# Seven PSUM banks in one pool, padded 128-row fills and 40 side chunks in a fused attention and gated-MLP kernel

## The chip, the cores and the metric

The kernel runs on one core of one Trainium2 chip. What counts is its time on the device in microseconds, the median of several runs. The core has five engines with instruction queues of their own: TensorE (PE in the profile; PEld are its weight loads), VectorE (DVE), ScalarE (ACT), GpSimd (POOL) and SyncE (SP, which here only issues DMAs). The engines run side by side and wait for each other on semaphores. Matmuls write into PSUM, which has eight banks of 128 x 512 fp32; VectorE and ScalarE read it from there, and in this kernel GpSimd reads and writes SBUF alone.

## The reference

```python
def _attn_ref(x, inducing):            # x (4, 12416, 128), inducing (32, 128)
    I = np.broadcast_to(inducing[None], (B, m, C))
    def mab(q, kv):
        s = scale * (q @ kv.transpose(0, 2, 1))
        s = s - s.max(-1, keepdims=True)
        a = np.exp(s)
        a /= a.sum(-1, keepdims=True) + 1e-09
        return a @ kv
    h = mab(I, x)                       # stage 1: 32 rows attend to all of x
    return mab(x, h)                    # stage 2: every row of x attends to the 32
def _moe_ref(x, w_gate, w_val, w_out): # 49664 tokens, d_ff = 1536
    gate = 1.0 / (1.0 + np.exp(-(x @ w_gate)))
    val = x @ w_val
    return gate * val @ w_out
```

Stage 2's result is `a2 @ h` with only 32 columns in `a2`, so the kernel multiplies `h` by the gate and value weights once for each batch (`hw`, 32 rows) and gets every hidden value as `a2 @ hw`. The sigmoid is written as (tanh(z/2) + 1) / 2, and the half is taken at the end.

## The kernel before

**Tiling.** The 49664 tokens are cut into 97 blocks of 512 tokens, 24 to a batch and one of left-over columns at the end. The hidden size of 1536 is 12 slices of 128. A *chunk* is one slice of one block, 128 x 512 hidden values, and there are 1164. For each chunk TensorE makes two *fills* of one PSUM bank each (`hidden_mm`, L1080): the gate values and the value part, with 32 rows of `hw` as weights. The two slices of a pair and the gate and value parts lie on four different groups of 32 rows, so up to four fills can run beside each other in the array. ScalarE takes tanh of the gate bank into a ring in SBUF (`issue_gate`, L1131), for one chunk or two at a time. VectorE makes the *product* (t + 1) * v from the ring and the value bank (`product`, L1276), again for one chunk (128x512) or two (128x1024). TensorE then multiplies the product by `w_out` in four matmuls of 128 columns (`out_mm`, L1218), which gather all 12 slices of a block in the bank `acc`. ScalarE evacuates that bank (L1333), and SP sends the block off (L1244).

**Banks.** The eight banks are given out by tags: two for double gate fills (`g2`), one for single ones (`g1`), two for the double value fills of every other step (`v2`), two for the steps between (`vm`), and one for `acc`. Of `vm`, the second bank also takes the small work of the two attention stages and of side chunks. So gate units of two chunks (letter `g`) and of one (`h`) take turns.

**Side chunks.** Nine chunks, in the blocks that `ASIDE` lists, go another way (`plan_aside`): ScalarE takes tanh into SBUF (L1187), GpSimd adds 1 (L1189), ScalarE copies the value bank into SBUF (L1192), and GpSimd multiplies (L1194). Their output matmuls come at the end of their block.

**The attention stages** run in the gaps. For each group of 2048 columns, stage 2 makes scores on TensorE (L624), ScalarE copies them out (L661), GpSimd takes the row maximum in a tree of pairwise steps and subtracts it (L671 to L676), ScalarE takes `exp` (L685), GpSimd sums in a tree (L693), inverts (L717 to L732) and spreads the result over four row groups (L739), and SP transposes it by DMA (L750) into `a2r`, which the fills read. Stage 1 of the next batch runs at the same time: scores, maximum (L386), `exp` (L399), transposing DMA (L423), weighted sums (L434).

**The order** is a string written out by hand or by a tool, `ORDER`: a letter is one step, and all engines get their instructions in the order in which the letters issue them. `V` and `W` fill value banks, `x` is a product, `o12` twelve output matmuls, `e` an evacuation by ScalarE (`f` by VectorE), `k7` or `K7` the next step of side chain 7. Side chains are the attention stages, loads and transposes of x, and the side chunks. Steps on one engine run in that order; a step that waits holds up what is behind it.

Of the kernel before, what the change touches and what calls it, by code (L numbers as in the profile page):

```python
# [10 lines left out]
F32 = mybir.dt.float32  # L11
F16 = mybir.dt.float16
# [10 lines left out]
    75, 79, 79, 86, 91, 91, 91, 95, 95,  # L23
# [13 lines left out]
RING = 16  # L37
ORDER = """
ghVxgVxk0hk0Vxgo4hVk0xo4Vxgo12Vxho4ghk72Vxo8k0gVxo4k0k74Vxho12Wxeghk76Vxo12gWxo4hk0Vxo4go4Vxho4g
k0k73Vxk1Vxho8k1k1k1gVxhVxo12Vxegk6Vk6xho16k6gk6Vxo8hWxo4ghk83Vxo4Wxgo8hVxo8Vxeghk8o8Vk8xgk8hVx  # L40
o16gk8Vxo4Wxho8gk75Vxo12ehWxgo12hk78Vxo4k7k1gVxo4k7k7hk1Vxo8gWxo8Vxho4gWxo8ehk1k77Vxgo12hWxo4go4
hVxo4k2gVxo4k2k1k80Vxk2k2ho8gWxo12VxehVxgk10o4hVk10xo4Vxgo4ho8Vxk10go8hWxo8gk10Vxo4ho4k9gVxk9Vx
o4k9ehgWxo8hk79k82Vxo8gVxk12o4hVk12xo4Vxgo4ho8k84Vxk12go12Wxehk12Vxgo8k18k2hVk18xo12k18gk2Vxo4hV
xo12k18Vk18xgo8hWxo4eghk2k81k85Vxo12k11Vxgk11hVxo12k11gVxo4hVxo4k3gVxo4k3k2Vxk3k3ho12WxegVxho12V
xgk14hVk14xo4Vxgo20Vxk14hgWxo12k14Vxehgo4k13Vxho4k13gVxo4Vxho12Vxk13go8hWxo4go4hVxo8egVxk16hVk16
xo8k16gVxo12k16Vxk3ho8k19Vxk19go4hk3Vxo8k15gVxk15Vxk15ho8egWxk3Vxho12k17gVxo4k17hVxo4k17gVxo12h
k3Vk20k20xo4k4Vxk4go12VxehWxgo12hVxo4go4k5hVxk5k5k5gVxo8k20hWxo8k20k86k87Vxgo12ehWxgo8Vxho8gWxo8
hVxo4go4Vxho4gVxo12VxehgVxo8hVxo8Vxk5ghVxo12k5Vxgo4hVxo4k20gVk20xo8Vk20xho4eghk5Vxk21Vxk21o8k21
k21gVxo8hWxo8gVxho12gWxo12ehk5VxgVxk20o8k20hVxo4gVxo8hVxo4gWxo4ho8gVxo4Wxho8eghVxo12gWxo4hk88Vx
o8gWxo8Vxk21hgo12k20Vxo4k20ehk21VxgWxo8ho4gk21k89Vxo8hWxo4go4hk21Vxo8gWxo12ehVxgo8Wxho8gVxo8hk22  # L50
gVxk22Vxho8k22k22gVxo4hVxo12WxeghVxo16gWxo8Vxho4ghWxo8gVxo12ehVxgo4Vxho8gWxo8hVxo8k22ghWxo16k22
k90VxgWxo4ehgk22Vxo12hWxo4go4k91Vxho8gWxho8gk22Vxo4Vxho8Vxegk23Vxho8k23k23k23gk92Vxo12hWxo4gVxo8
ho4gWxo12ehk93Vxgk28o8Vk28xho8Vxk28go4Wxho4k28Vxgo8hWxo4go8hk94Vxo4Vxegk30ho12Vk30xgk30hVxo8k30V
xgo4Wxho8gk95Vxo4hk29Vxk29k29gVxho12Wxegk96Vxho16k31k23gVxo4hk23Vxk31o8k31gVxhVxo8gWxo4k23Vxho8e
# [40 lines left out]
def kernel(  # L95
# [184 lines left out]

    vm = []
    joined = {}
    OTHER = {"v1": "m", "m": "v1"}

    here = {"bank": "m"}

# [14 lines left out]
    def bank(tag, shape, dtype, name):  # L301
        if tag == "m":
            tag = here["bank"]
# [1065 lines left out]
```

## Time and profile before

| what | value |
|---|---|
| median of 3 runs | 714.05 us (713.93 to 714.75) |
| the profiled execution: its own time | 713.77 us |
| its span, first to last instruction | 712.0 us |
| granted TensorE clock | 1.0 throughout |
| products (L1276) | 484 for two chunks, 187 for one |
| tanh into the ring (L1131) | 385 for two chunks, 385 for one |
| side chunks | 9 |
| evacuations by ScalarE (L1333) | 96 |

How the profile's rows are read: a group's row has the source line, the engine, the operation, its output and input tiles with shapes, and how often it occurs; behind the first bar the busy time in us and the mean duration of one in ns; behind the second the time that the engine stood idle just ahead of them, and what ended it. A row of the waits has in us the total, how often, and the longest. A row of the timeline has start and duration in us. Consecutive instructions of DVE or ACT overlap: the next starts before the row of the last has ended, so what a step costs its engine is read from start to start.

### The profile page before, as it was taken

What the parts mean: (1) busy time and instruction counts of PE and PEld (TensorE: products, weight loads), DVE (VectorE), ACT (ScalarE), POOL (GpSimd) and SP (SyncE); (2) the same over time, 40 slices, a digit from 0 to 9 for tenths busy, and PEclk for the clock granted to TensorE, in tenths of its full rate; (3) what the DMA queues carried; (4) which work ended last, traced back from release to release, by engine and by line L of the source; (5) the groups of instructions that cost most, each with busy time, mean ns of one, the idle gap of its engine ahead of it and who ended that gap; (6) DMA issues with size and microseconds to landing.
All of it is one profiled execution on the core that took longest, in us unless ns stands there. A gap on an engine that the chain in (4) does not pass through costs nothing.

```text
span 712.0 us, 21058 instructions
## 1 busy us (share of the span) xinstructions
PE 681.4 (96%) x8446; PEld 402.0 (56%) x8446; DVE 697.3 (98%) x773; ACT 679.1 (95%) x1019; POOL 446.0 (63%) x718
## 2 busy tenths in 40 slices
PE   8899999999999999999999999999999999999997
PEld 4455565555555555555555555555555555555555
DVE  6899999999999999999999999999999999999997
ACT  4699999999999999999999999999999999999996
POOL 4574663788763747578766266378766788766220
PEclk9999999999999999999999999999999999999999
DMA  9796775244459353325258631220222222023011
GB/s 212 116 175 136 144 142 114 75 91 107 90 126 172 65 120 84 69 75 122 49 131 156 116 76 53 70 73 33 77 61 47 74 61 76 31 75 77 31 46 46
DMA packets 118178, 65.73 MB, mean 92 GB/s; under 512 B 101408, under 2 KB 102208, under 8 KB 118080
## 3 DMA queue, kind: packets, MB, share of 16 engines
q1 hardware_dynamic: 112176, 50.90, 30.4%
q0 software_dynamic: 5584, 13.34, 11.2%
q8 instruction: 66, 1.08, 0.7%
q14 instruction: 32, 0.26, 0.1%
q10 hardware_dynamic: 320, 0.15, 0.1%
HBM read 27.80 MB, written 25.43 MB: 75 GB/s over the span
## 4 chain that ended last, share of the span: by engine, by line
PE 46%; ACT 23%; DVE 20%; issue 8%; DMA 2%; POOL 1%; DVEq 0%; ACTq 0%; POOLq 0%
PE acc_ps L1218 22%; DVE u L1276 18%; ACT t L1131 18%; PE g_ps L1080 12%; PE vm_ps L1080 5%; PE v_ps L1080 4%; ACT o L1333 3%; DMA xn<-in_x_dram 2%; PE vm_ps L624 1%; PE vm_ps L434 1%; ACT sc L661 1%; ACT a1T L399 1%; DVE nm L386 1%; ACT e L685 0%; PE vm_ps L1177 0%
## 5 line engine op out<-in xcount | busy, mean ns | idle before, releaser
L1131 ACT ACTIVATE t<-g_ps 128x1024 f16<-128x1024 f32 (+1 forms) x770 | 587.8, 819 | 10.6 <-PE g_ps L1080 2.0
L1276 DVE SCALAR_TENSOR_TENSOR u<-t,v_ps 128x1024 f16<-128x1024 f16 (+1 forms) x337 | 407.6, 1210 | 0.9 <-PE v_ps L1080 0.3
L1218 PE MATMUL acc_ps<-wo,u 128*128 128x128 f16 x4596 | 364.4, 220 | 4.8 <-ACT o L1333 0.9
L1218 PEld LDWEIGHTS <-u 128*128 128x128 f16 x4620 | 262.5, 98 | 153.6 <-issue 146.3
L1276 DVE SCALAR_TENSOR_TENSOR u<-t,vm_ps 128x1024 f16<-128x1024 f16 (+1 forms) x335 | 307.6, 918 | 0.4 <-PE vm_ps L1080 0.2
L1080 PE MATMUL g_ps<-a2r,hwt 32*128 32x512 f16 (+1 forms) x1179 | 286.5, 375 | 5.1 <-ACT t L1131 0.4
L1080 PEld LDWEIGHTS <-hwt 32*128 32x128 f16 x2382 | 98.5, 91 | 116.8 <-issue 47.1
L1080 PE MATMUL v_ps<-a2r,hwt 32*128 32x512 f16 (+1 forms) x687 | 129.3, 373 | 5.2 <-DVE u L1276 3.7
L1080 PE MATMUL vm_ps<-a2r,hwt 32*128 32x512 f16 (+1 forms) x492 | 129.0, 376 | 5.0 <-DVE u L1276 3.2
L693 POOL TENSOR_TENSOR sum<-e 128x256 f32<-128x256 f16 (+1 forms) x23 | 15.5, 673 | 121.2 <-ACT e L685 117.8
L739 POOL TENSOR_TENSOR a2n<-e,rs 128x2048 f16<-128x2048 f16 (+3 forms) x25 | 86.8, 3474 | 5.1 <-DVE rs L711 3.4
L717 POOL TENSOR_TENSOR near<-sme,minus 128x16 f32<-128x16 f32 (+1 forms) x22 | 65.2, 2966 | 1.7
L1333 ACT ACTIVATE o<-acc_ps 128x512 f32<-128x512 f32 x96 | 57.8, 602 | 0.7 <-ACT t L1131 0.2
L672 POOL TENSOR_SCALAR rise<-rise 128x256 f32<-128x256 f32 (+6 forms) x110 | 51.2, 465 | 9.7
L671 POOL TENSOR_TENSOR rise<-sc 128x256 f32<-128x256 f32 (+1 forms) x22 | 16.2, 738 | 27.2 <-ACT sc L661 27.1
L673 POOL TENSOR_TENSOR top<-top,rise 128x128 f32<-128x128 f32 (+3 forms) x88 | 28.4, 323 | 7.3
L693 POOL TENSOR_TENSOR sum<-sum 128x128 f32<-128x128 f32 (+3 forms) x92 | 28.5, 309 | 7.2
L671 POOL TENSOR_TENSOR rise<-top 128x128 f32<-128x128 f32 (+3 forms) x88 | 27.3, 310 | 6.9
L1194 POOL TENSOR_TENSOR xn_spare<-xn_spare 128x512 f16<-128x512 f32 x9 | 11.4, 1270 | 22.5 <-ACT xn_spare L1192 22.3
L676 POOL TENSOR_TENSOR sc<-sc,top 128x512 f32<-128x512 f32 (+1 forms) x22 | 23.9, 1086 | 1.7
L1189 POOL TENSOR_SCALAR xn_spare<-xn_spare 128x512 f32<-128x512 f16 x9 | 13.4, 1492 | 18.3 <-ACT xn_spare L1187 18.2
L624 PE MATMUL vm_ps<-hT,xT 128*128 128x32 f16 x376 | 17.5, 177 | 0.6 <-DVE u L1276 0.3
(165 smaller groups left out, 328.2 us busy)
## 6 DMA issues: line engine op xcount, KB each, us to landing
out_dram<-o SPq DMA_DIRECT2D x96, 256.0 KB, 2.3
xn<-in_x_dram POOLq DMA_DIRECT2D x18, 512.0 KB, 6.0
xn<-in_x_dram POOLq DMA_DIRECT2D x3, 544.0 KB, 6.5
xn<-in_x_dram POOLq DMA_DIRECT2D x3, 256.0 KB, 12.1
xn<-in_x_dram SPq DMA_DIRECT2D x1, 576.0 KB, 4.8
xn<-in_x_dram SPq DMA_DIRECT2D x1, 512.0 KB, 3.9
a2r<-a2n SPq DMA_TRANSPOSE x29, 4.5
wg<-in_moe_w_gate_dram POOLq DMA_DIRECT2D x1, 384.0 KB, 12.2
```

The lines of the kernel that those rows point to most:

```text
L624: on("m", nc.tensor.matmul(s2[:, j, :], xT[b][:, c + j, :], hT16[b][:], start=(j == 0), stop=whole and j == j1 - 1, skip_group_check=True,))
L671: nc.gpsimd.tensor_tensor(out=r, in0=far, in1=near, op=ALU.subtract)
L672: nc.gpsimd.tensor_scalar_max(out=r, in0=r, scalar1=0.0)
L673: nc.gpsimd.tensor_tensor(out=top[:, 0:n, 0:w], in0=near, in1=r, op=ALU.add)
L693: nc.gpsimd.tensor_tensor(out=d[:, 0:n, :], in0=src[:, :, 0:w], in1=src[:, :, w : 2 * w], op=ALU.add)
L717: nc.gpsimd.tensor_tensor(out=near[:, 0:n], in0=sme[:, 0:n], in1=minus1[:, 0:n], op=ALU.pow)
L739: eng.tensor_tensor(out=a2n[:, 0:n, :, :], in0=e.unsqueeze(2).to_broadcast((P, n, 4, m)), in1=rs.unsqueeze(2).unsqueeze(3).to_broadcast((P ...
L1080: made_mm.append(nc.tensor.matmul(out[:, col : col + nb * P], hw[b][r : r + 32, j // 2, :], a2r[r : r + 32, o : o + nb, :].rearrange("p j ...
L1131: i = nc.scalar.activation(out=ring[:, p : p + n, :], in_=g[:, 0:n, :], func=AF.Tanh, scale=0.5)
L1218: mm = nc.tensor.matmul(acc[0][half][:, i, :], u[:, ts(i, P)], wo16[:, j, :], start=(i in fresh), stop=not left[ib] and not any(e[1] == ib ...
L1276: x = nc.vector.scalar_tensor_tensor(out=u[:, 0:n, a:e], in0=ring[:, p : p + n, a:e], scalar=1.0, in1=v[:, 0:n, a:e], op0=ALU.add, op1=ALU ...
L1333: evac.pop()(lambda out, in_, by: nc.scalar.mul(out=out, in_=in_, mul=by))
```

## The change

1. The eight banks are now one tile of seven banks (`vm`) and `acc`. Each gate and value fill names its banks in the order itself: `g01` fills banks 0 and 1 with gate values of two chunks, `v4` bank 4 with the value part of one. A side chain's step that takes a bank is written with a capital (`A` to `G` are banks 0 to 6). `on` no longer parts two banks but keeps, bank by bank, who used it last, and makes each user wait for that one alone.
2. Some fills are padded to 128 rows: `p` and `q` for gate and value fills, capitals `H` to `N` for side chains. Their weights are a copy of `hw` in which the 96 other rows are zero, and they read all 128 rows of `a2r`. GpSimd makes these weights once for each batch (`make_alone`) in a part of `xT` that stage 2 has done with: one memset of 128 x 3072 and four copies of 32 x 768. 218 fills are padded.
3. `ASIDE` lists 40 chunks instead of 9, from block 7 on instead of block 75.
4. The order is drawn anew. It has 464 products for two chunks and 196 for one, 444 tanhs into the ring for two and 236 for one, 90 evacuations by ScalarE and six (`f`) by VectorE. The places in the ring are counted round 15, with a sixteenth for a pair that would straddle the end.

The core of the diff:

```diff
 ASIDE = (
-    75, 79, 79, 86, 91, 91, 91, 95, 95,
+    7, 11, 12, 13, 24, 24, 26, 27, 32, 34, 36, 38, 48, 50, 51, 51, 53, 56, 58, 59, 61, 64, 68,
+    70, 75, 75, 79, 79, 79, 82, 84, 86, 86, 89, 90, 91, 91, 91, 95, 95,
 )
...
-ghVxgVxk0hk0Vxgo4hVk0xo4Vxgo12Vxho4ghk72Vxo8k0gVxo4k0k74Vxho12Wxeghk76Vxo12gWxo4hk0Vxo4go4Vxho4g
+g01C0k0g3v45k0g6xg0g3v1v65xg4g0o8xg1v34o4g56v0k0g1xxv34o4k74v0g56o12k0v2xg34v56xg10xxo8v23g4o12
...
+    def on(where, i, keep=()):
+        if vm:
+            banks = frozenset((here["bank"],) if where == "m" else where)
             me = str(i.ins.engine)
...
+            for (others, who), group in seen.items():
+                if who != me and not others & banks:
+                    tc.declare_no_dep(i.ins, group=group, keep=list(keep), reason="another bank")
...
+            after = {}
+            for k in banks:
+                for who, x in reversed(users.setdefault(k, [])):
+                    if who == me:
+                        break
+                    after.setdefault(x.name, x)
+                    if who == PE:
+                        break
+                users[k] = [(who, x) for who, x in users[k] if who != me] + [(me, i.ins)]
+            for name in after:
+                tc.add_manual_dep(i.ins, name, AFTER, reason="the bank's use before this one")
...
-    vm.append(ps.tile([P, 2, 512], F32, tag="vm", name="vm_ps"))
+    vm.append(ps.tile([P, 7, 512], F32, tag="vm", name="vm_ps"))
...
+    def make_alone(b):
+        w = xT[b][:, NLO : NLO + 4 * NI, :]
+        nc.gpsimd.memset(w, 0.0)
+        for r in range(4):
+            q = slice(32 * r, 32 * r + 32)
+            nc.gpsimd.tensor_copy(out=w[q, NI * r : NI * r + NI, :], in_=hw[b][q])
+        alone[b] = w
+
+    def weights(what, b, j, whole):
+        r = j % 2 + (2 if what == "v" else 0)
+        if whole:
+            return alone[b][:, NI * r + j // 2, :], slice(0, P)
+        q = slice(32 * r, 32 * r + 32)
+        return hw[b][q, j // 2, :], q
...
+    def fill_unit(what, c, banks, whole):
+        home = sorted(banks)
+        for k in banks:
+            j = c + home.index(k)
+            made_hw = [x for b, _, _ in blocks[chunks[j][0]] for x in joined.get(b, ())]
+            for i in hidden_mm(what, j, vm[0][:, k, :], whole):
+                on((k,), i, made_hw)
+        return span(vm[0], home)
...
-        g = ps.tile([P, n, 512], F32, tag=f"g{n}", name="g_ps")
-        for k in range(n):
-            hidden_mm("g", c + k, g[:, k, :])
...
+        g = fill_unit("g", c, banks, whole)
...
-        v = vm[0] if half else ps.tile([P, 2, 512], F32, tag="v2", name="v_ps")
...
+        ready.append((fill_unit("v", c, banks, whole), banks))
```

What the new table makes of the engines' queues is shown with the prediction, at the places that it speaks of: ScalarE and GpSimd around the third group of stage 2 of the first batch, and TensorE a third of the way through.

More of the change, by code (lines that the diff above doesn't have):

```diff
@@ L309, in bank @@
         size = 1
[L310 to L311 removed]
+        for n in shape[1:]:
+            size *= n
         flat = flat[:, 0:size]
```

390 lines of the change are left out of this document (211 added, 179 removed).

## The prediction

> **What bounds the kernel now.** I read the page, then the busy times by stretch, what VectorE (DVE) waited for, its products by shape, and last the timeline of one stretch. First the page's span, its busy line and engine shares of the chain that ended last, the ordered part from 40 to 690 us in the stretch view (length, then PE, PEld, DVE, ACT, POOL busy), and two rows of DVE's waits.
>
> ```profile
> span 712.0 us, 21058 instructions
> PE 681.4 (96%) x8446; PEld 402.0 (56%) x8446; DVE 697.3 (98%) x773; ACT 679.1 (95%) x1019; POOL 446.0 (63%) x718
> PE 46%; ACT 23%; DVE 20%; issue 8%; DMA 2%; POOL 1%; DVEq 0%; ACTq 0%; POOLq 0%
> 40.00:690.00 650.00, 629.02 (x7750) 370.42 (x7747) 649.33 (x678) 638.70 (x949) 425.91 (x675) 1.00 0.41 90
> DVE u L1276 <- PE v_ps L1080: 0.3, 1, 0.3
> DVE u L1276 <- ACT t L1131: 0.3, 1, 0.3
> ```
>
> Three engines look full, but only DVE is: for 650 us it stands still 0.7 us, and its two waits on the products are 0.3 us each. The chain passes through TensorE, ScalarE and DVE because they hand banks round in a ring; it doesn't name the bound. So the cost of one DVE step is what counts, from one start to the next. Its products by shape, then a stretch of the timeline (start, duration):
>
> ```profile
> L1276 DVE SCALAR_TENSOR_TENSOR u<-t,v_ps 128x1024 f16<-128x1024 f16 x335 | 406.8, 1214 | 0.9 <-PE v_ps L1080 0.3 <-ACT t L1131 0.3
> L1276 DVE SCALAR_TENSOR_TENSOR u<-t,vm_ps 128x1024 f16<-128x1024 f16 x149 | 181.0, 1215 | 0.2
> L1276 DVE SCALAR_TENSOR_TENSOR u<-t,vm_ps 128x512 f16<-128x512 f16 x186 | 126.6, 681 | 0.2 <-PE vm_ps L1080 0.2
> 304.04 1.22 DVE L1276 SCALAR_TENSOR_TENSOR u<-t,v_ps 128x1024 f16<-128x1024 f16 x1
> 305.17 0.68 DVE L1276 SCALAR_TENSOR_TENSOR u<-t,vm_ps 128x512 f16<-128x512 f16 x1
> 305.77 1.21 DVE L1276 SCALAR_TENSOR_TENSOR u<-t,v_ps 128x1024 f16<-128x1024 f16 x1
> 306.90 1.22 DVE L1276 SCALAR_TENSOR_TENSOR u<-t,vm_ps 128x1024 f16<-128x1024 f16 x1
> ```
>
> Rows overlap by 0.08 us: a double product holds DVE 1.13 us (305.77 to 306.90), a single one 0.60 (305.17 to 305.77). There are 484 doubles and 187 singles (the last is cut in two).
>
> **The change, part by part.** *DVE.* Counted in the new table, 464 doubles and 196 singles are left for 1124 chunks, and six evacuations (`f`) come to DVE. The nearest row for one of those has half its width:
>
> ```profile
> L1235 DVE TENSOR_SCALAR o<-vm_ps 128x256 f32<-128x256 f32 x1 | 0.4, 425 | 0.3 <-PE vm_ps L1218 0.3
> ```
>
> At double width it adds what 256 columns add to a product, 0.27: 0.69, or 0.61 from start to start. DVE: -20 x 1.13 + 9 x 0.60 + 6 x 0.61 = **-13.5 us**, all on the path.
>
> *ScalarE* (ACT). Its groups, then a stretch without a wait:
>
> ```profile
> L1131 ACT ACTIVATE t<-g_ps 128x1024 f16<-128x1024 f32 x385 | 397.0, 1031 | 9.8 <-PE vm_ps L1080 1.9 <-PE g_ps L1080 1.9 <-PE v_ps L1080 1.3
> L1131 ACT ACTIVATE t<-g_ps 128x512 f16<-128x512 f32 x385 | 233.4, 606 | 0.8 <-PE g_ps L1080 0.2
> L1333 ACT ACTIVATE o<-acc_ps 128x512 f32<-128x512 f32 x96 | 57.8, 602 | 0.7 <-ACT t L1131 0.2
> L1187 ACT ACTIVATE xn_spare<-vm_ps 128x512 f16<-128x512 f32 x9 | 5.4, 601 | 0.0
> L1192 ACT COPY xn_spare<-vm_ps 128x512 f32<-128x512 f32 x9 | 5.3, 586 | 0.0
> 102.85 1.02 ACT L1131 ACTIVATE t<-g_ps 128x1024 f16<-128x1024 f32 x1
> 103.77 0.58 ACT L661 COPY sc<-vm_ps 128x512 f32<-128x512 f32 x1
> 104.23 0.61 ACT L1131 ACTIVATE t<-g_ps 128x512 f16<-128x512 f32 x1
> 104.72 0.62 ACT L1333 ACTIVATE o<-acc_ps 128x512 f32<-128x512 f32 x1
> 105.20 1.54 ACT L1131 ACTIVATE t<-g_ps 128x1024 f16<-128x1024 f32 x2
> ```
>
> From start to start a double tanh is 0.92, a single 0.49, a copy 0.46, an evacuation 0.48. The new table has 444 doubles and 236 singles. With 31 more side chunks (a tanh and a copy each): 59 x 0.92 - 149 x 0.49 + 31 x 0.95 - 6 x 0.48 = **+7.9 us**. Priced so, the 949 ACT steps between 40 and 690 need about 614 of 650 us; the rest of its 638.7 "busy" is ends that nothing overlapped. After: 622 of 650 - 13.5 = 636.5, where DVE needs all: 97.7% where it was 94.5%. On ACT, around the third `exp` (`e<-sc`) of the first batch; `xn` is a side chunk's room; before, then after:
>
> ```order
> L399 ACTIVATE a1T<-vm_ps,nm_1_143 128x512
> L1131 ACTIVATE t_621<-g_ps 128x1024
> L685 ACTIVATE e<-sc 128x512
> L1131 ACTIVATE t_621<-g_ps 128x512
> L449 COPY hst_146<-vm_ps 32x129
> L1131 ACTIVATE t_621<-g_ps 128x1024
> ```
>
> ```order
> L1257 ACTIVATE xn_1632<-vm_ps 128x512
> L1262 COPY xn_1632<-vm_ps 128x512
> L1202 ACTIVATE t_619<-vm_ps 128x1024 x3
> L1407 ACTIVATE o_2141<-acc_ps 128x512
> L490 COPY hst_146<-vm_ps 128x129 x2
> L1257 ACTIVATE xn_1632<-vm_ps 128x512
> L727 ACTIVATE e<-sc 128x512
> L1202 ACTIVATE t_619<-vm_ps 128x512
> L1262 COPY xn_1632<-vm_ps 128x512
> ```
>
> Where double and single tanhs took turns, three doubles now stand in a row, and two side chunks stand close together, one of them round the `exp`; every tanh behind them in ACT's queue comes later by their 1.9 us, which the tanhs ahead of DVE must cover. If they don't, the 1.9 us stand on the path.
>
> The six `f` evacuations hand their output transfers to SP after DVE instead of ACT; an output is waited for by nothing but the end, so I cost that at nothing (256 KB each; if SP's queue stood behind one, the transposes in it would come later by a product, 1.13).
>
> *GpSimd* (POOL). A side chunk's two steps, the bounds for the padded weights, and its two largest waits:
>
> ```profile
> L1189 POOL TENSOR_SCALAR xn_spare<-xn_spare 128x512 f32<-128x512 f16 x9 | 13.4, 1492 | 18.3 <-ACT xn_spare L1187 18.2
> L1194 POOL TENSOR_TENSOR xn_spare<-xn_spare 128x512 f16<-128x512 f32 x9 | 11.4, 1270 | 22.5 <-ACT xn_spare L1192 22.3
> L218 POOL MEMSET ones<- 128x128 f32 x1 | 0.2, 224 | 0.0
> POOL sum L693 <- ACT e L685: 117.8, 19, 14.3
> POOL rise L671 <- ACT sc L661: 27.1, 12, 3.5
> ```
>
> 31 x 2.76 = 86 us. A batch's padded weights (a memset of 3072 columns, four copies of 768) lie between 5 x 0.22 = 1.1 us and 6144 columns at 1492/512 ns = 17.9; I take 5.5, nearer the memset, as nothing is computed: 22 us for four. POOL goes from 446 to about 554 of 700; the 145 us in the two waits cover the 108. On POOL behind the third maximum tree (which ends in `sc`), before, then after:
>
> ```order
> L676 TENSOR_TENSOR sc<-sc,top 128x512
> L693 TENSOR_TENSOR sum_2522<-e 128x256
> L693 TENSOR_TENSOR sum_2524<-sum_2522 128x128
> L693 TENSOR_TENSOR sum_2526<-sum_2524 128x64
> L693 TENSOR_TENSOR sum_2528<-sum_2526 128x32
> ```
>
> ```order
> L718 TENSOR_TENSOR sc<-sc,top 128x512
> L1259 TENSOR_SCALAR xn_1632<-xn_1632 128x512
> L1264 TENSOR_TENSOR xn_1632<-xn_1632 128x512
> L1259 TENSOR_SCALAR xn_1632<-xn_1632 128x512
> L735 TENSOR_TENSOR sum_2245<-e 128x256
> L735 TENSOR_TENSOR sum_2247<-sum_2245 128x128
> ```
>
> 4.3 us of side work (1.49 + 1.27 + 1.49) stand where POOL waited for `exp`. Behind them queue the sums and the spread, behind those on SP the transposing DMA that later fills wait for, and behind the last of them in PE's queue the side chunk's own output products, with every fill after those. The side chunks of the first two batches use the room of `xn` of the batches after next, so the loads into it, which POOL issues, wait for those products; they are needed a batch later, some 170 us, and cost nothing unless POOL stands on them. The Trainium skill (GPSIMD Engine Reference, 4.1 Engine selection) speaks against this: elementwise work belongs on VectorE, GpSimd being about 2x slower with two inputs and near line rate with one. The trace has the one-input step slower (1.49) than the two-input one (1.27); priced by the page, 0.53 + 1.2 instead of 2.76, the 86 us would be some 54, and the end would not move.
>
> *TensorE* (PE). Fills and output products (start, duration), and the only 128-row matmuls of 512 columns near them:
>
> ```profile
> 300.25 0.40 PE L1218 MATMUL acc_ps<-wo,u 128*128 128x128 f16 x4
> 300.58 0.39 PE L1080 MATMUL g_ps<-a2r,hwt 32*128 32x512 f16 x2
> 300.78 0.39 PE L1080 MATMUL v_ps<-a2r,hwt 32*128 32x512 f16 x2
> 301.10 0.62 PE L1218 MATMUL acc_ps<-wo,u 128*128 128x128 f16 x8
> 301.65 0.39 PE L1080 MATMUL g_ps<-a2r,hwt 32*128 32x512 f16 x1
> 29.22 0.82 PE L329 MATMUL w_ps<-xT,ident 128*128 128x512 f16 x3
> ```
>
> Three padded-size matmuls take 0.82 - 0.39 = 0.43 up to the last start: 0.22 each. 128 columns cost (0.55 - 0.33) / 4 = 0.055; four and a change of shape 0.33, so a change is 0.11, and two 32-row fills up to the next change 0.32 = 0.22 + 0.10. Walked over PE's order, the changes fall from 1370 to 1189 (-18 us), and 218 of 2304 fills become padded, which run alone: were all to ride beside another now, +48; by the walk they give back the 18 and 2 more (609 us before, 611 after). Either way PE needs under 640 of 698, hidden by DVE. The Trainium skill (TensorEngine Tiling (Array Packing), Tiling Modes, Key Properties) says that a change of tiling mode drains TensorE; the trace agrees, at 0.11 a change. Also, waits for a bank now stand on the weight load. PE a third of the way through, with the engine that each waits for, before, then after (`xT` holds padded weights, `hwt` the old ones):
>
> ```order
> L1080 LDWEIGHTS hwt
> L1080 MATMUL g_ps<-a2r,hwt 128x512 [waits Activation_49]
> L1080 LDWEIGHTS hwt
> L1080 MATMUL g_ps<-a2r,hwt 128x512
> L1080 LDWEIGHTS hwt
> L1080 MATMUL v_ps<-a2r,hwt 128x512 [waits DVE_49]
> ```
>
> ```order
> L1145 LDWEIGHTS xT_97 [waits DVE_49]
> L1145 MATMUL vm_ps<-a2r,xT_97 128x512
> L1145 LDWEIGHTS xT_97
> L1145 MATMUL vm_ps<-a2r,xT_97 128x512
> L1145 LDWEIGHTS xT_97 [waits Activation_49]
> L1145 MATMUL vm_ps<-a2r,xT_97 128x512
> ```
>
> All four fills are padded here, and some 1400 waits moved to the loads; behind each stands the whole PE queue, as before. A load that waited, in before:
>
> ```profile
> 40.40 0.11 PEld L1218 LDWEIGHTS <-u 128*128 128x128 f16 x2 [0.36 <-DVE u L1276]
> 40.41 0.23 PE L1218 MATMUL acc_ps<-wo,u 128*128 128x128 f16 x1 [0.19 <-DVE u L1276]
> ```
>
> Its matmul followed 0.01 us later: a load that may not run ahead costs between 0 (it can't gain) and its row's 0.11, and I take 0.01, the row that shows it. Only stalled fills pay it, and PE's spare 87 us hide it.
>
> **The sum.** 712.0 - 13.5 = 698.5 span, + 1.8 around it (713.8 - 712.0) = 700.3 if DVE stays as full. By needs in stretches of 24 chunks, ACT or PE now tops DVE in 8 of 48 stretches, by 2.9 us together, of which DVE lost 0.7; after, in 14 of 47, by 9.3: a quarter is 2.2, and 1 us for late GpSimd work: **703.5 us**. The run is 0.3 under the median of 714.05.
>
> **The rivals.** *ACT becomes the bound* (22%). The best stretch of before:
>
> ```profile
> 550.00:650.00 100.00, 96.73 (x1120) 56.70 (x1116) 99.92 (x102) 99.13 (x148) 77.88 (x116) 1.00 0.23 61
> ```
>
> Its 148 ACT steps, priced as above, fill 96.6%, with DVE still full. If that is the most that ACT can be fed, its 622 us take 643.9 instead of 636.5: 707.7, and at 96% 711.7. For it: a tanh can't start before PE has refilled a bank that ACT or DVE has just left, and the banks are as many as before (seven besides the accumulator's). Against: in before DVE's pace held ACT back, so 96.6% is no limit that it ran into, and 149 fewer single tanhs mean fewer hand-overs.
>
> *GpSimd is late, and the kernel slower* (13%). The margin of an `exp` behind its tree:
>
> ```profile
> 507.14 1.08 POOL L676 TENSOR_TENSOR sc<-sc,top 128x512 f32<-128x512 f32 x1
> 509.61 0.63 ACT L685 ACTIVATE e<-sc 128x512 f16<-128x512 f32 x1
> ```
>
> The tree ended at 508.22, 1.4 us before. The added 108 us of POOL are 4.9 for each of 22 groups. If ACT stands 1.6 at each `exp`, a third of that, the tanhs queued behind it lose 35 us; ACT's spare 14.5 takes some, 20.5 are left, and less the 13.5 won it is 7 slower: 721. It decides from (14.5 + 13.5) / 22 = 1.3 us per `exp`. For it: the margin is small already, and ACT has little to catch up with. Against: the order was redrawn, and POOL's waits hold more than the added work.
>
> *It doesn't do what it says* (7%): the seven banks are one tile, and where a fill still waits for another bank's user the two rings fall into step; by a wait of half a product's time at one in 24 products, 27 x 0.57 = 15, the gain is gone: 714. *All of it fits* (8%): the stretches cost nothing and DVE's rows close up: 699.5.
>
> **The numbers.** The forecast has 50% and by itself reaches from 700 (nothing lost) to 707 (7 of the stretches' 9.3 us paid in full). From 699 to 712.5 the range takes in it, the full gain and ACT as the bound, 80%; it leaves out no change and the slower case. A measurement tells 0.2% (1.4 us): faster 0.80, same 0.07, slower 0.13.
>
> **What would show it.** Right: 464 and 196 products at the old durations, DVE near 684 us busy and idle for under 4 between 40 us and the last 20; 444 and 236 main tanhs; POOL near 550 us; PE below DVE. ACT as the bound would show as DVE waiting for `t`, late GpSimd work as ACT's `exp` waiting for `sc` or output products waiting for `xn`, a load that costs as DVE waiting for fills. What would make the forecast wrong is several us of any of these three, or products that became slower beside a busier GpSimd.

## The result, and the profile after

The changed kernel takes 709.26 us (median of 4 executions, 708.05 to 710.49), the kernel before, measured beside it, 713.99; the ratio is 0.9932 (95% interval 0.9911 to 0.9954). It is 4.7 us faster, where 10.5 were forecast. The profiled execution took 708.05 us, the shortest of the four. First the page of the changed kernel: span, engines, shares of the chain that ended last; then the stretch view from 40 to 690 us and two of DVE's waits.

```profile
span 706.2 us, 21185 instructions
PE 679.1 (96%) x8446; PEld 402.2 (57%) x8446; DVE 687.7 (97%) x768; ACT 676.7 (96%) x985; POOL 553.2 (78%) x800
PE 62%; ACT 18%; DVE 9%; issue 5%; DMA 4%; POOL 1%; DVEq 0%; ACTq 0%; POOLq 0%
40.00:690.00 650.00, 632.97 (x7817) 374.68 (x7817) 645.46 (x679) 641.56 (x919) 531.47 (x755) 1.00 0.41 90
DVE u L1344 <- ACT t L1202: 1.4, 2, 1.2
DVE u L1344 <- PE vm_ps L1145: 0.9, 3, 0.4
```

DVE no longer fills the stretch: it stands for 4.54 us (650 - 645.46) where it stood for 0.67. The chain has moved from DVE (20% to 9%) to TensorE (46% to 62%). The groups of DVE and ACT by shape, and GpSimd's padded weights:

```profile
L1344 DVE SCALAR_TENSOR_TENSOR u<-t,vm_ps 128x1024 f16<-128x1024 f16 x463 | 539.9, 1213 | 2.9 <-PE vm_ps L1145 0.9
L1344 DVE SCALAR_TENSOR_TENSOR u<-t,vm_ps 128x512 f16<-128x512 f16 x196 | 129.3, 679 | 1.5 <-ACT t L1202 1.4
L1409 DVE TENSOR_SCALAR o<-acc_ps 128x512 f32<-128x512 f32 x6 | 4.1, 686 | 0.0
L1202 ACT ACTIVATE t<-vm_ps 128x1024 f16<-128x1024 f32 x444 | 441.8, 1046 | 6.9 <-PE vm_ps L1145 3.8
L1202 ACT ACTIVATE t<-vm_ps 128x512 f16<-128x512 f32 x236 | 139.2, 623 | 1.3 <-PE vm_ps L1145 0.5
L1129 POOL COPY xT<-hwt 32x768 f16<-32x768 f16 x16 | 13.1, 818 | 0.8
L1126 POOL MEMSET xT<- 128x3072 f16 x4 | 10.6, 2658 | 0.2
```

463 doubles and the cut last one, 196 singles, six `f`, all at the old durations: DVE's work fell as forecast. So 13.5 us of work went and 5.8 of span. DVE's busy sum fell by only 9.6 (697.3 to 687.7): a product whose successor comes late shows its last 0.08 us as busy, which an overlapped one hides. By this reckoning 13.5 - 9.6 = 3.9 us of overlap were lost, and DVE stood still 3.9 us more. That is 7.8 us, where the sum had 3.2.

The 7.8 us are mostly short stops. One of them, in TensorE's and then DVE's part of the timeline (start, duration):

```profile
441.29 1.05 PE L1288 MATMUL acc_ps<-wo,u 128*128 128x128 f16 x16
442.27 0.40 PE L1145 MATMUL vm_ps<-a2r,hwt 32*128 32x512 f16 x4
441.98 0.68 DVE L425 TENSOR_REDUCE nm<-vm_ps 128x1 f32<-128x512 f32 x1
442.80 2.35 DVE L1344 SCALAR_TENSOR_TENSOR u<-t,vm_ps 128x1024 f16<-128x1024 f16 x2
```

DVE's reduction ended at 442.66, the product began at 442.80: its fill stood behind 16 output products in TensorE's queue. The longest stop is another. Its rows are SP's issues, the wait of TensorE and the spreads on GpSimd; the first fence is the changed kernel, the second the kernel before, where the same transposition went out ten us sooner:

```profile
209.25 8.02 SPq L197 DMA_TRANSPOSE xT<-xn  x3
218.49 1.22 SPq L464 DMA_TRANSPOSE a<-a1T  x1
219.80 1.93 SPq L792 DMA_TRANSPOSE a2r<-a2n  x1
210.65 3.61 POOL L781 TENSOR_TENSOR a2n<-e,rs 128x2048 f16<-128x2048 f16 x1
PE vm_ps L1145 <- DMA a2r<-a2n: 1.0, 1, 1.0
```

```profile
206.02 3.61 POOL L739 TENSOR_TENSOR a2n<-e,rs 128x2048 f16<-128x2048 f16 x1
209.66 1.90 SPq L750 DMA_TRANSPOSE a2r<-a2n  x1
```

The spread ended 4.6 us later than before (214.26 to 209.63), behind the side chunks on GpSimd, and then its DMA was issued only 5.5 us later (219.80): SP's queue still held the last of the three transposing DMAs of the input (to 217.27), an output and a transposing DMA of weights (`a<-a1T`). TensorE waited 1.0 us at 224 us, ACT for it, and DVE for ACT: the 1.2 in DVE's first wait above.

### The profile page after: what moved, and what is told of

It reads as the page before. It is cut to its first block, busy times and chain, and to the rows that moved or that the text cites. A ratio compares the mean times of both kernels' runs of the same rounds, so it can differ in the third digit from the quotient of the medians.

```text
span 706.2 us, 21185 instructions
## 1 busy us (share of the span) xinstructions
PE 679.1 (96%) x8446; PEld 402.2 (57%) x8446; DVE 687.7 (97%) x768; ACT 676.7 (96%) x985; POOL 553.2 (78%) x800
## 4 chain that ended last, share of the span: by engine, by line
PE 62%; ACT 18%; DVE 9%; issue 5%; DMA 4%; POOL 1%; DVEq 0%; ACTq 0%; POOLq 0%
PE acc_ps L1288 30%; PE vm_ps L1145 27%; ACT t L1202 14%; DVE u L1344 8%; ACT o L1407 2%; PE vm_ps L1247 2%; DMA xn<-in_x_dram 2%; PE vm_ps L666 1%; DMA xT<-xn 1%; DMA a2r<-a2n 1%; PE vm_ps L413 0%; ACT xn_spare L1262 0%; ACT sc L703 0%; PE vm_ps L475 0%; DMA a<-a1T 0%
## 5 line engine op out<-in xcount | busy, mean ns | idle before, releaser
L1344 DVE SCALAR_TENSOR_TENSOR u<-t,vm_ps 128x1024 f16<-128x1024 f16 (+2 forms) x661 | 651.6, 1053 | 4.4 <-ACT t L1202 1.4
L1202 ACT ACTIVATE t<-vm_ps 128x1024 f16<-128x1024 f32 (+1 forms) x680 | 557.3, 899 | 8.2 <-PE vm_ps L1145 4.3
L1145 PE MATMUL vm_ps<-a2r,hwt 32*128 32x512 f16 (+1 forms) x2103 | 281.6, 377 | 12.1 <-DVE u L1344 4.4
L1145 PEld LDWEIGHTS <-hwt 32*128 32x128 f16 x2127 | 82.3, 91 | 114.8 <-ACT t L1202 29.5
L1145 PE MATMUL vm_ps<-a2r,xT 128*128 128x512 f16 x193 | 62.6, 382 | 1.5 <-DVE u L1344 0.4
L1259 POOL TENSOR_SCALAR xn_spare<-xn_spare 128x512 f32<-128x512 f16 x28 | 41.8, 1494 | 17.2 <-ACT xn_spare L1257 16.9
L1264 POOL TENSOR_TENSOR xn_spare<-xn_spare 128x512 f16<-128x512 f32 x28 | 35.6, 1270 | 19.1 <-ACT xn_spare L1262 10.5
L1145 PEld LDWEIGHTS <-xT 128*128 128x128 f16 x193 | 16.3, 97 | 17.2 <-DVE u L1344 5.4
L1259 POOL TENSOR_SCALAR xn<-xn 128x512 f32<-128x512 f16 x12 | 17.9, 1495 | 8.0 <-ACT xn L1257 7.7
L1247 PE MATMUL vm_ps<-a2r,hwt 32*128 32x512 f16 x55 | 20.1, 383 | 0.3 <-DVE u L1344 0.2
```

The lines of the kernel that those rows point to most:

```text
L1145: made_mm.append(nc.tensor.matmul(out[:, col : col + nb * P], w, a2r[q, o : o + nb, :].rearrange("p j t -> p (j t)"), start=True, stop=True,))
L1202: i = on(banks, nc.scalar.activation(out=span(ring, spots), in_=g, func=AF.Tanh, scale=0.5), [x for q in old for x in product_of[q]])
L1247: on("m", nc.tensor.matmul(st[what], w, a2r[q, o : o + nb, :].rearrange("p j t -> p (j t)"), start=True, stop=True,))
L1259: nc.gpsimd.tensor_scalar_add(out=st["t1"], in0=st["t"], scalar1=1.0)
L1264: nc.gpsimd.tensor_tensor(out=st["t"], in0=st["t1"], in1=st["v32"], op=ALU.mult)
L1344: x = on(banks, nc.vector.scalar_tensor_tensor(out=u[:, 0:n, a:e], in0=t[:, :, a:e], scalar=1.0, in1=v[:, :, a:e], op0=ALU.add, op1=ALU.mu ...
```

## The experiments

There were three theories at the start: the way of a bank through TensorE (release, load, fill) has become too long, ACT is full, or GpSimd's work comes late. Gains below are against the kernel before on the same chip, and "more" or "less" against the 4.5 us of `again`.

| run | median us | ratio to before (95%) | before less run |
|---|---|---|---|
| again | 709.36 | 0.9928 (0.9912 to 0.9945) | 4.5 |
| waits_on_matmuls | 711.13 | 0.9967 (0.9950 to 0.9984) | 2.7 |
| no_padded_fills | 717.47 | 1.0045 (1.0032 to 1.0059) | -3.6 |
| short_pool_steps | 707.85 | 0.9913 (0.9896 to 0.9930) | 6.0 |
| transposes_apart | 709.39 | 0.9944 (0.9929 to 0.9960) | 4.7 |
| products_496 | 706.91 | 0.9901 (0.9888 to 0.9913) | 7.2 |
| tanhs_496 | 712.07 | 0.9975 (0.9961 to 0.9988) | 2.0 |
| half_columns | 680.81 | 0.9542 (0.9507 to 0.9578) | 33.3 |
| transposes_later | 709.93 | 0.9935 (0.9913 to 0.9956) | 4.2 |
| fewer_out_products | 710.12 | 0.9938 (0.9914 to 0.9962) | 4.0 |
| tanhs_496_again | 707.86 | 0.9919 (0.9894 to 0.9945) | 6.2 |
| half_columns_of_before | 658.11 | 0.9214 (0.9199 to 0.9230) | 56.0 |
| calm | 711.29 | 0.9962 (0.9948 to 0.9977) | 3.0 |
| both_496 | 700.96 | 0.9808 (0.9791 to 0.9824) | 13.3 |
| half_short_pool | 662.41 | 0.9292 (0.9252 to 0.9332) | 51.9 |
| half_no_padded | 684.00 | 0.9584 (0.9566 to 0.9602) | 30.3 |
| loads_swapped | 708.45 | 0.9913 (0.9898 to 0.9927) | 5.7 |
| loads_swapped_waits_on_matmuls | 707.04 | 0.9909 (0.9896 to 0.9921) | 7.1 |

**again** (no edit)

> The changed kernel as it is, to have its time from more executions than four and a second trace beside which the others can be read. 709.3 us within 1, by every theory. If DVE's stops between 40 and 690 us fall in the same places as in the first trace (near 114, 227, 442, 487, 521 us), they belong to the order; if they fall elsewhere, to the execution.

The time repeats, and the stops lie in the same places, but for one more: 1.4 us at 231. The stretch view of this second trace around it, in steps of 2 us (length, busy PE, PEld, DVE, ACT, POOL with their instructions, granted clock, DMA share, GB/s):

```profile
224.00:226.00 2.00, 0.93 (x14) 0.46 (x11) 1.35 (x2) 0.63 (x2) 1.83 (x4) 1.00 1.21 166
226.00:228.00 2.00, 2.00 (x14) 0.62 (x12) 1.40 (x3) 1.97 (x3) 1.75 (x4) 0.84 0.80 169
228.00:230.00 2.00, 2.00 (x15) 1.13 (x15) 1.62 (x2) 1.86 (x3) 1.59 (x6) 0.50 0.00 0
230.00:232.00 2.00, 2.00 (x60) 1.10 (x61) 1.02 (x1) 1.19 (x3) 1.59 (x6) 0.81 0.00 0
232.00:234.00 2.00, 2.00 (x58) 1.18 (x47) 2.00 (x4) 2.00 (x6) 0.63 (x1) 1.00 0.32 116
```

Behind the pause at 224 (TensorE busy 0.93 of 2 us) the granted clock falls to 0.50. The missing clock is 2 x (0.16 + 0.50 + 0.19) = 1.7 us, so half clock for 3.4 us; DVE loses 0.98 us from 230 to 232 alone. Product by product, the second trace is 1.4 us behind the first after this place and within 0.1 us of it everywhere else. In the first trace the pause was 1.0 us instead of 1.07, and the clock stayed at 1.00. This also parts the nine executions of the changed kernel (both groups): with a granted clock of 0.999 or 1.0 they took 707.59, 708.05, 708.52 and 708.97 us, with 0.996 to 0.998 they took 709.36 to 710.49; the means are 1.6 us apart. The page on TensorE in the Trainium skill (TensorE: Matmul & The Clock Gate, Part 1: The HAM clock gate (the "warmup" mystery)) has the half rate and a window of some 3.4 us, which agrees; it has the clock fall after an idle window of that length, and here a pause of 1.07 us was enough.

**waits_on_matmuls**

```diff
-            for name in after:
+            for name in after if me != PE else ():
                 tc.add_manual_dep(i.ins, name, AFTER, ...)
```

> Every fill's wait for its bank stands on its matmul, as in the kernel before, and no longer on the weight load ahead of it; the order of all engines, the banks and the padded fills are those of the changed kernel. Theory of the loop (a bank that comes free has to pass the load, then the fill, then the tanh or product, and the load's share of about 0.06 us now lies on that way; in the trace DVE stops 43 times for a fill and 13 times for its own release of the bank, 6.7 us together where it was 1.7 before): the stops fall by about 4 us, to 705 us, and ACT's waits for fills shorten with them. Rival, ACT is full (its steps need 622 of 650 us, so a fill that comes sooner finds ACT busy): 709 within 0.7. Rival, late GpSimd work: 709 within 0.5.

1.8 us less was won, not 4 more: the load on the way is not what holds the fills up (the table further down has 0.5 us for it at full clock). In its trace the pause at 224 us was 1.5 us, with half clock behind it, and a second one of 1.1 stood at 112 us; all seven executions had a clock of 0.992 to 0.997.

**no_padded_fills**

```diff
-            fill_value(banks, word == "q")
+            fill_value(banks, False)
...
-            issue_gate(banks, word == "p")
+            issue_gate(banks, False)
...
-            take_step(int(k), TAKES.index(word) % 7, TAKES.index(word) >= 7)
+            take_step(int(k), TAKES.index(word) % 7, False)
```

> All fills with 32 rows and the old weights, none padded; GpSimd still makes the padded weights, so that its queue stays what it was. Order and banks as in the changed kernel. The changes of shape on PE rise again where a padded fill stood between output products. Theory of the loop: a fill that stands alone between 128-row work pays two changes of 0.11 us, so the 218 padded ones were worth up to 0.2 us each on PE, and DVE stops more: 711 to 714. Rival, the padded fills themselves are what comes late (they run alone at 0.22 where two 32-row fills run side by side): 706 to 707.

8.1 us less, slower than the kernel before. The rival falls: without its 218 padded fills the new order is no faster than the old one. The stretch view of this kernel:

```profile
40.00:690.00 650.00, 624.97 (x7709) 363.76 (x7708) 638.18 (x669) 634.82 (x909) 529.20 (x753) 0.99 0.41 89
```

DVE stands 11.8 us. Part of it is clock: behind a pause of 1.45 us at 226 it was at 0.50 for 10.2 us in all; the twelve executions had 0.987 to 0.996. Of the 9.8 us by which this trace's span is longer than that of the changed kernel, 4.0 fall there and 3.5 behind it, at full clock.

**short_pool_steps**

```diff
-            nc.gpsimd.tensor_scalar_add(out=st["t1"], in0=st["t"], scalar1=1.0)
+            nc.gpsimd.tensor_scalar_add(out=st["t1"][:, 0:128], in0=st["t"][:, 0:128], scalar1=1.0)
...
-            nc.gpsimd.tensor_tensor(out=st["t"], in0=st["t1"], in1=st["v32"], op=ALU.mult)
+            nc.gpsimd.tensor_tensor(out=st["t"][:, 0:128], in0=st["t1"][:, 0:128], in1=st["v32"][:, 0:128], op=ALU.mult)
```

> GpSimd's two steps of a side chunk cover 128 of its 512 columns (three quarters of the add and the product of the 40 side chunks are left out), about 2.0 us less in each of 40, 80 us in all; every queue keeps its order. Theory of late GpSimd work (the transposing DMA that PE waited 1.0 us for at 225 us, the exps that start 0.2 to 0.5 us behind their tree): 1.5 to 3 us faster, 706.5 to 708, and the stop near 227 us gone. Loop through PE, or ACT full: within 0.7 of the changed kernel but for that one stop (1.25 us).

1.5 us more, at the edge of what was expected and with an interval that overlaps that of `again`. The pause at 224 us is still there (1.05 us): the spread ended at 213.1 us, 1.1 sooner, and its DMA was issued at 219.45 all the same, behind the same queue of SP.

**transposes_apart**, **transposes_later**, **calm**, **loads_swapped**: only steps of DMAs move in `ORDER` (`k92` to `k95` transpose the third batch's input, `k80` and `k82` load the second's).

```diff
 transposes_apart
-...C120xk94k93k92k28e...   ...k30k121xv4g01...       ...k29g34o4v2...
+...C120xk94k28e...         ...k30k121xk92v4g01...    ...k29g34k93o4v2...
 transposes_later
-...C120xk94k93k92k28e...   ...o8k95g23...   ...k30v43xg01...      ...k29g34o4v2...      ...o16v56g2...
+...C120xk94k28e...         ...o8g23...      ...k30v43k92xg01...   ...k29g34k93o4v2...   ...o16v56k95g2...
 calm: transposes_later and
-...g2o12xxk2v0...       ...k9v23k82eg45...   ...xg65k80o8k2...
+...g2o12xk82k80xk2v0... ...k9v23eg45...      ...xg65o8k2...
 loads_swapped: transposes_later and
-...k9v23k82eg45...   ...xg65k80o8k2...
+...k9v23k80eg45...   ...xg65k82o8k2...
```

> Of the three transposing DMAs of the third batch's input that stand in a row on SP near 209 us (8.0 us to issue), two stand behind the spread's transposing DMA (a2r<-a2n) and the next step's; nothing else moves. In the trace that a2r was ready to go at 214.3 us (end of its spread on GpSimd), issued at 219.8, and TensorE waited for it 1.0 us at 225, after which DVE stood 1.25 us (1.3 and 1.4 us in two places in the second trace). Theory of late DMAs: those stops go, 1.3 to 2.7 us faster, 706.7 to 708.1. Theory that TensorE's own room is what lacks: the time saved is lost again at the next tight place, within 0.7 of 709.3.

No change (0.2 us more). The a2r was in time, but the transposition of the next step's weights, behind the moved DMAs, was late: TensorE waited 1.4 us at 229 us and DVE stood 1.4.

> As transposes_apart, but the input's transposing DMAs (two of the three that stood in a row, and the next one) now stand behind the spread's a2r and behind both transposing DMAs of the next batch's weights (a<-a1T), one of which was late in transposes_apart (TensorE waited 1.4 us for it at 229 us, and DVE stood 1.4 us). Theory: TensorE's pause near 225 us and, in the executions that have it, the half clock behind it are gone: 706.7 to 708 us, and the executions lie closer together. Rival: the order there is so tight that another step is late in its place: 709 within 0.7.

At the median no change (0.3 less), but the two executions at full clock took 707.59 and 707.93, and the place at 225 us is free; the others, at 0.990 to 0.997, took 708.73 to 712.0. In its trace 1.3 us are won there and 1.1 lost at a pause of 0.96 us near 105 us, where TensorE waits for the second batch's transposed input. The edit moves nothing ahead of 205 us, so the place at 105 us is late in some executions and not in others.

> The changed kernel with the order of DMAs alone moved: two loads of the second batch's input stand ahead of the maximum tree on GpSimd's queue (they were issued at 88 and 92 us, 8 us later than in the kernel before, and TensorE waited 1.0 and 3.4 us for their transposition in two traces), and the third batch's transposing DMAs as in transposes_later. Theory of late DMAs and the half clock: no pause of TensorE over 0.9 us, granted clock 1.00 in every execution, 707 to 708 us. Rival, coupling of full engines alone: still 709 within 0.7.

The loads in question on GpSimd, in the changed kernel and in the kernel before (start, duration; the expectation misread them: the second batch's last two went out at 83.7 and 88.4 us, those at 91.7 are the third batch's):

```profile
83.70 0.64 POOL L188 DMA_DIRECT2D xn<-in_x_dram  x1
88.41 0.61 POOL L188 DMA_DIRECT2D xn<-in_x_dram  x1
```

```profile
74.45 0.64 POOL L158 DMA_DIRECT2D xn<-in_x_dram  x1
83.68 1.15 POOL L158 DMA_DIRECT2D xn<-in_x_dram  x2
```

The theory's forecast failed: 1.5 us less. The loads, put ahead of the maximum tree, made the spread's a2r late: issuing it beside them took SP 5.6 us from 75.2 us on, where the changed kernel took 2.1. TensorE's wait at 83 us, and the stretch view:

```profile
PE vm_ps L1145 <- DMA a2r<-a2n: 2.5, 1, 2.5
84.00:86.00 2.00, 0.16 (x3) 0.10 (x2) 0.67 (x1) 0.00 (x0) 0.91 (x1) 0.93 1.11 318
86.00:88.00 2.00, 2.00 (x15) 1.00 (x13) 1.22 (x1) 1.14 (x2) 0.00 (x0) 0.50 0.86 281
88.00:90.00 2.00, 2.00 (x16) 1.20 (x12) 1.22 (x1) 2.00 (x4) 1.44 (x1) 0.50 0.03 8
90.00:92.00 2.00, 2.00 (x18) 0.99 (x16) 1.22 (x1) 1.07 (x2) 1.87 (x3) 0.50 0.00 0
92.00:94.00 2.00, 2.00 (x24) 0.97 (x20) 1.11 (x2) 1.23 (x2) 1.57 (x6) 0.87 0.00 0
```

The price of a late transfer can be read here: a wait of 2.5 us, then 6.8 us of half clock (3.4 missing), and DVE at 1.11 to 1.22 of 2 us for four steps, 3.2 us lost behind the wait.

> transposes_later, and two loads of the second batch's input exchanged on GpSimd's queue: the one whose transposition TensorE waited for near 105 us is issued at 83.7 us instead of 88.4, and the other, needed later, at 88.4. Late transfers as the cause of the scatter: no pause over 0.6 us at 105 and 225 us, granted clock 1.00 in most executions, median 707 to 708. Rival: the lateness turns up elsewhere as in calm, 709 to 711.

1.2 us more; at 708.45 the median lies between the two forecasts, and the pause at 105 us is still there (0.92 us). Three executions at 0.999 took 705.87, 706.91 and 707.69, three at 0.995 and 0.996 took 709.20 to 709.54. The half clock was not gone: in the trace it stood from 607.1 to 610.5 us, behind no pause over 0.6 us but a stretch with few matmuls (16 from 604 to 606, where 23 to 33 stood in the steps of 2 us before).

**loads_swapped_waits_on_matmuls** (loads_swapped with the edit of waits_on_matmuls)

> loads_swapped, with each fill's wait for its bank on the matmul instead of the weight load. If waits_on_matmuls lost its 1.8 us only by longer pauses and the half clock behind them (its executions lie at granted clocks of 0.992 to 0.997), this one is within 1 us of loads_swapped or up to 1.5 faster. If the place of the wait itself costs, it is 1 to 2 us slower than loads_swapped.

The lowest time of an unabridged kernel, 707.04: 7.1 us under the kernel before, 2.6 more than `again`, 1.4 more than loads_swapped (the intervals overlap). So the load ahead of the wait costs little, and waits_on_matmuls lost by its pauses: 1.9 us in its trace at the one of 224 us.

**products_496**, **tanhs_496**, **both_496**, **fewer_out_products**: less work for one engine at a time, then for two. tanhs_496_again has `nc.vector.memset` instead; both_496 has both edits and needs no memset.

```diff
 products_496
-        cuts = [0, 384, 512] if final else [0, 512]
+        cuts = [0, 384, 496] if final else [0, 496]
...
-            u[:, ts(i, P)],
+            u[:, min(P * i, 368) : min(P * i, 368) + P],
 tanhs_496
+    nc.gpsimd.memset(ring[:, :, 496:512], 0.0)
...
-            out=span(ring, spots), in_=g, func=AF.Tanh, scale=0.5
+            out=span(ring, spots)[:, :, 0:496], in_=g[:, :, 0:496], func=AF.Tanh, scale=0.5
 fewer_out_products
+        if i == 3 and j % 2 and not (i in fresh or stop or final):
+            return
```

> The products cover 496 of 512 columns (16 are left out; an output product reads the last 128 columns that were computed), which takes 16 x 0.53/512 = 0.017 us from each of 1124 chunks, 18.6 us of DVE; nothing else changes. Theory that DVE still sets the end and only loses some stops: 15 us or more faster, 691 to 694. Theory that TensorE (with ACT) sets the pace as much as DVE: under 6 us faster, 703 to 708.

18.6 us less of DVE win 2.7 (the intervals just touch): DVE no longer sets the end by itself. The stretch view of this kernel:

```profile
40.00:690.00 650.00, 631.49 (x7822) 373.19 (x7823) 636.46 (x680) 641.67 (x922) 530.68 (x755) 1.00 0.42 90
```

DVE stands 13.5 us where it stood 4.5, and ACT is as busy as before (641.67 to 641.56).

> The main tanhs cover 496 of 512 columns (16 of each chunk stay at zero), 16 x 0.43/512 = 0.0134 us from each of 1124 chunks, 15 us of ACT, so that ACT needs 607 of 650 as in the kernel before or less. Theory that ACT is full and passes its lateness on: 3 to 6 us faster, 703 to 706. Theory that TensorE's fills are what comes late, not ACT: under 1.5 us faster.

This run was spoilt by its own memset: the first product waited 2.8 us for it, and the clock was half from 34 to 41 us.

> As tanhs_496, with the zeros of the 16 columns written by DVE instead of GpSimd, where the first product waited 2.8 us for them at 30 us and TensorE's clock was half until 41 us. 15 us less of ACT in the ordered part. ACT full: 703 to 706. TensorE: under 1.5 us faster, 708 to 709.5.

1.7 more for 15 us less of ACT, with an interval that overlaps that of `again`: ACT alone doesn't set it either.

> 510 of the 4472 output products are left out (the last quarter of the rows of every second block of hidden units, but for the first and the last of a group), 510 x 0.055 = 28 us of TensorE; every tanh, product, fill and wait stays. Theory that TensorE sets the pace beside DVE (half_columns: 680.8 us with half the work of ACT and DVE): DVE's stops for fills fall to about a third, 4 to 7 us faster, 702 to 705. Rival, that the stops are the length of the way from a bank's release through load and fill, not TensorE's load: under 2 us faster.

0.5 less for 28 us less of TensorE, so the 4 to 7 us of the theory did not come, and the rival's under 2 us hold. The executions had 0.985 to 0.995; in the trace 6.8 us of half clock stood behind a pause of 1.0 us near 113 us, and 2.7 us were lost there. At full clock, behind 247.5 us, 1.8 were won: TensorE's load is a small part of it.

> Tanhs and products both cover 496 of 512 columns (16 are left out), 15 us less of ACT and 18.6 less of DVE. products_496 alone won 2.5 us, tanhs_496_again 1.5. Theory of coupled full engines (ACT, DVE and TensorE each within a few per cent): more than the sum of both, 8 to 14 us faster, 695 to 701. Rival, that TensorE and the DMAs set the pace, or fixed lengths of the way: no more than the sum, 705 to 708.

8.8 us more, twice the sum of the two alone (2.7 + 1.7). The stretch view of this kernel:

```profile
40.00:690.00 650.00, 632.72 (x7920) 376.23 (x7920) 639.11 (x685) 636.07 (x928) 532.41 (x756) 1.00 0.43 90
```

It stays within the coupled theory's range (701). DVE stands 10.9 us even so; TensorE is at 632.7 as before. That the engine which is relieved alone waits for the banks that the other hands over fits this, and is argued.

Pauses and half clock can be left out of the comparison: from the 211th product, at 247.5 us in the first trace, to the last one, 453.7 us later, none of the traces below has a pause of TensorE over 0.6 us or any half clock. The table has how much longer (or shorter, -) each takes from that product to the last.

| run | us against the first trace |
|---|---|
| again, calm, transposes_later, transposes_apart | 0.06, 0.07, 0.15, 0.35 |
| short_pool_steps (80 us less of GpSimd in the whole kernel) | -0.10 |
| waits_on_matmuls, loads_swapped_waits_on_matmuls | -0.48, -0.42 |
| products_496 (18.6 less of DVE) | -0.77 |
| tanhs_496, tanhs_496_again (15 less of ACT) | -1.25, -1.95 |
| fewer_out_products (28 less of TensorE) | -1.79 |
| both_496 | -6.42 |
| no_padded_fills | 3.47 |

The first row, with nothing left out, tells the scatter. Here too DVE and ACT together win 6.4 us, where DVE alone wins 0.8 and ACT alone 1.25 and 1.95. Relieved alone, an engine stands while the other stays full: in tanhs_496_again ACT stands 8.9 of the 440 us from 250 to 690 and DVE 1.9, where the first trace has 4.6 and 2.5 from 247.5 to 690.

**half_columns**, **half_columns_of_before**, **half_short_pool**, **half_no_padded**: tanhs and products over half their columns, so that the rest sets the time. half_short_pool has the edit of short_pool_steps besides, half_no_padded that of no_padded_fills.

```diff
-            out=span(ring, spots), in_=g, func=AF.Tanh, scale=0.5
+            out=span(ring, spots)[:, :, 0:256], in_=g[:, :, 0:256], func=AF.Tanh, scale=0.5
...
-        cuts = [0, 384, 512] if final else [0, 512]
+        cuts = [0, 128, 256] if final else [0, 256]
...
-            u[:, ts(i, P)],
+            u[:, min(P * i, P) : min(P * i, P) + P],
```

> Tanhs and products cover 256 of 512 columns (half is left out; output products read the columns that were computed), so that ACT and DVE need some 240 and 300 us less, while TensorE has every fill and output product of the changed kernel in the same order: the time is what TensorE needs by itself, with the start and the end. Theory of the prediction (TensorE needs 611 us, 87 spare): 620 to 650. Theory that TensorE's room is what lacks (its drains at changes of shape, walked at 0.11 each, are longer): 675 to 705.

> The kernel before with tanhs and products over 256 of 512 columns (half is left out): what TensorE needs by itself for the old order. By the walk of the prediction (609 us before, 611 after) within 4 us of half_columns (680.8). If the padded fills and the new order took load off TensorE, longer by what they took off, 10 us or more; if the padded fills are a load, shorter.

> half_columns (half of every main tanh and product left out) with GpSimd's two steps of a side chunk over 128 of 512 columns as well, 80 us less of GpSimd. Theory that the 22.7 us by which half_columns is longer than half_columns_of_before are GpSimd's added work and what waits for it (TensorE waited 5.1 us there for side chunks' products): 660 to 668. Rival, that it is TensorE's own work in the new order: 677 to 681.

> half_columns with 32-row fills only, none padded (GpSimd still makes the padded weights). What the padded fills are to TensorE where DVE and ACT have time: if they are a load (218 at 0.22 that run alone), 3 to 15 us faster than half_columns, 666 to 678; if they save it changes of shape, as no_padded_fills (8.1 slower) suggests, slower than 683.

The engines' busy line and the chain of each page show what bounds them: half_columns, then half_short_pool, then half_columns_of_before.

```profile
PE 642.5 (95%) x8446; PEld 385.7 (57%) x8446; DVE 431.7 (64%) x768; ACT 483.8 (72%) x985; POOL 553.0 (82%) x800
POOL 43%; PE 41%; DMA 7%; issue 5%; ACT 3%; DVE 1%; POOLq 0%; ACTq 0%; SPq 0%; DVEq 0%
```

```profile
PE 636.6 (97%) x8446; PEld 384.1 (58%) x8446; DVE 431.8 (66%) x768; ACT 483.8 (73%) x985; POOL 483.2 (73%) x800
PE 74%; POOL 10%; DMA 7%; ACT 4%; issue 3%; DVE 1%; SPq 0%; ACTq 0%; POOLq 0%; DVEq 0%
```

```profile
PE 631.9 (97%) x8446; PEld 377.5 (58%) x8446; DVE 436.7 (67%) x773; ACT 470.9 (72%) x1019; POOL 445.9 (68%) x718
PE 69%; POOL 14%; ACT 6%; DMA 6%; issue 3%; DVE 1%; ACTq 0%; SPq 0%; POOLq 0%; DVEq 0%
```

With little for DVE and ACT to do, TensorE paces the old order at 658.1 us and the new one, once GpSimd is relieved, at 662.4. As it is, the new order takes 680.8, with GpSimd and TensorE on the chain: 18.4 of the 22.7 us between the orders are its side chunks. These medians are rough, as the executions of the two kernels in the new order spread over 8 to 9 us at clocks of 0.984 to 1.0. Without padded fills it is 684.0, 3.2 longer, but the intervals overlap and the clock was lower (0.975 to 0.982), so this doesn't show that they save time here too.

## Why the forecast was wrong

- **DVE, -13.5 us**: right, in number and duration. Busy 687.7 and idle 4.5, where 684 and under 4 were named, are the lost overlap and the stops.
- **ACT**: the counts came as read from the table, and its 622 us of need stand in 650 - 5.8 = 644.2 us, 96.6%. That is the figure of the rival in which ACT becomes the bound, whose 707.7 to 711.7 hold the result. Its sign did not come (two waits for `t`, 1.4 us, 1.2 of them the late a2r), and 15 us off ACT alone win only 1.7. With DVE relieved too, the same 15 us win 6.1 (13.3 - 7.2): ACT is as much a bound as DVE, not the bound in its place. Its reason, that a tanh can't start before TensorE has refilled a bank that ACT or DVE has left, goes for DVE as well.
- **GpSimd, 446 to 554, 22 of them for the padded weights, 1 us late**: right in the work (553.2, 23.7); the 1 us is near the 1.2 of the late a2r, and three quarters of the side steps won 1.5, not clear of noise. "Cost nothing unless POOL stands on them" was the point to follow: the last loads of the second batch's input went out at 83.7 and 88.4 us instead of 74.5 and 83.7, one spread at 210.7 instead of 206.0, and what had been in time by a few us no longer was.
- **TensorE under 640 of 698, 87 us spare**: wrong in size. Left nearly to itself TensorE takes 658 to 662 us, so its room is some 47 of 709 (709.4 - 662.4), and GpSimd's in this order some 28 (709.4 - 680.8). A change of shape at 0.11 and a padded fill at 0.22 make unpadded fills 2 us shorter for TensorE (181 fewer changes at 0.11 are 20 us, where it wrote 18); the runs have the kernel 8.1 us longer with them, 3.5 of it at full clock. But TensorE's load is not what cost most of the time, as 28 us less of it won 1.8 in the 453.7 us of the table above.
- **The wait on the load, 0 to 0.11**: right that next to nothing of it reaches the end (0.5 us in those 453.7 us).
- **Sum, +2.2 for the stretches and +1 for GpSimd**: this is the step that failed, by its size. Priced stretch by stretch against the one engine on top, and a quarter of that, it came to 3.2 and was 7.8. What the runs showed in its place is that DVE and ACT bind together: relieved alone they won 2.7 and 1.7 us, together 8.8, and of a cut in one of them alone little comes back. On top of that comes the half clock, 1.6 us between the executions at full clock and the others, which the forecast did not know. The result stays inside the range because the range was wide enough for ACT as the bound, not because these terms were right.
- **The rival of the slower side**: GpSimd was late, but at DMAs, not at `exp`; none of ACT's waits for `sc` was among the long ones.

The six `f` evacuations were not tried alone. Open is how the 7.8 us divide: 1.2 are the late a2r of the profiled execution; for the rest both_496 shows a coupling of DVE and ACT, not how much of it each queue makes. That the half clock follows each late transfer is not so: pauses of 1.0 to 2.1 us stood without it (1.38 in transposes_apart, 2.13 in half_short_pool at 211 us), and which executions have it was not settled.

## What to carry to other kernels

When the busiest engine is relieved, find out how near the next ones are with a kernel that halves the work of the engines on top, not by adding up rows: here that puts TensorE 47 us and GpSimd 28 us behind, where the rows said 87 and 146 (700 - 554). Where two engines are both close to full, as DVE and ACT are here, relieve them one at a time and then together before you say what either is worth. Where an added step delays a queue, follow the transfers issued behind it to the first one that arrives with no margin, on GpSimd and on SP. A repair of one late transfer is worth a run of its own, as it can make another late.

## What the hardware showed unexpectedly

TensorE's granted clock fell to 0.50 behind pauses of TensorE from 1.0 us (fewer_out_products) to 4.0 (half_no_padded), for 3.4 us (again), 6.8 (calm) and 10.2 (no_padded_fills), and once behind a mere lack of matmuls (loads_swapped). In every trace that has it more than once, its starts lie whole multiples of 3.413 us apart (37.91, 109.59 and 710.33 us in tanhs_496_again: 21 and 197 of them), on a grid whose place differs from trace to trace. How a pause falls on that grid may matter: the longest one without half clock, in half_short_pool, is cut in two by it, and in `again` and the first trace the step of the grid that held the whole pause had 20 and 21 matmuls. That the matmuls within a step decide is not shown.
